# Block-sparse attention and a top-2 mixture of experts: the sums of the exponentials shared out between GpSimd and VectorE, with further sums ahead of TensorE

## The chip, the cores and the metric

The kernel runs on one core of a Trainium2 chip. The core has TensorE for matrix products (PE in the profile; PEld is its loading of weights), VectorE (DVE), ScalarE (ACT) and GpSimd (POOL), each with its own queue of instructions, executed in order; SyncE (SP) issues DMA transfers only. ScalarE and GpSimd issue some transfers too. The metric is the time on the device in microseconds, the median of several runs; lower is better.

## The reference, cut to what matters

Four batches of eight heads attend over 768 rows of width 64. Then each of the 3072 rows, 512 wide, goes through its two best of eight experts.

```python
scores = scale * np.matmul(q, k.transpose(0, 1, 3, 2))
scores = np.where(mask, scores, -1000000000.0)
scores = scores - np.max(scores, axis=-1, keepdims=True)
attn = np.exp(scores)
attn = attn / (np.sum(attn, axis=-1, keepdims=True) + 1e-09)
attn_out = np.matmul(attn, v)
x = attn_out.transpose(0, 2, 1, 3).reshape(B * S, H * D)
# router: noisy logits of x, the two best experts of each row, their weights
# experts: out[row] += weight * (relu(x[row] @ w1[e]) @ w2[e])
```

What the change touches is the sum over the exponentials, the epsilon, and the maximum on its way into the exponent.

## The kernel before, in words

**Attention.** Two heads make a group. A head has six chunks of 128 keys, one for each step: 192 steps in all, written out by `Attention.steps`. In step n TensorE forms the transposed scores of one chunk against all 768 queries in two halves (tile `pe`, L237 and L238: high and low parts of q and k in float16, and the maximum and the mask as further columns of the second product). ScalarE turns them into exponentials (tile `p`, float32, L239, five buffers). Four steps later TensorE multiplies them with the values (tile `po`, L269).

The maximum of each query is found ahead of time. TensorE forms the scores the other way round (tile `pm`, two buffers, L208), VectorE reduces them (`m`, L215), up to eleven chunks ahead of the step. When a head's six maxima are there, `max_end` writes them, scaled and in float16, into a column of `qb` on VectorE (L222); one step later SyncE transposes `qb` into `q2` (L225), which L238 of that head uses. The first heads have less lead than eleven chunks.

**The sums.** `add` (L257) lets GpSimd add the exponentials of two neighbouring chunks into a tile `acc`, 128 x 768: three pair sums for each head. `sums` (L280) then lets TensorE add those three, and the 128 keys within each, by matmuls with a constant column: four matmuls of 192 columns for each of the three, beside each other in four column groups of the array. ScalarE copies the result (`sb`, L297), VectorE transposes it (L300), adds epsilon (`rc`, L302) and takes the reciprocal (L305). TensorE turns the product with the values back (L310), VectorE scales it (`xr`, L313), ScalarE and GpSimd split it into two float16 parts (`x`, L322, L324).

Buffers tie the engines: an exponential needs a free `p`, freed by its pair sum and its product with the values; a product `pm` needs the reduction two before it done.

**Other work in the same queues.** GpSimd forms the low parts of k and q for later groups (L175, L179). The router of each batch runs in pieces in the steps of the next: some forty small VectorE instructions, then 48 writes to the table `slots` over the four batches, twelve a batch, each a small memset and an indirect DMA on GpSimd (L651, L652). The third batch's twelve stand closer together than those of the first two. Near the end of the attention GpSimd gathers the rows of the first expert (L771).

**Experts.** Units of up to 816 rows: two products on TensorE (L823, L843), ScalarE and VectorE between them, results scattered by GpSimd (L890). The fourth batch's router and table writes run beside the first unit.

Of the kernel before, what the change touches and what calls it, by code (L numbers as in the profile page):

```python
# [9 lines left out]
F32 = mybir.dt.float32  # L10
# [29 lines left out]
class Attention:  # L40
# [10 lines left out]
    PPB = 5  # L51
    LA = 4

    def __init__(self, tc, q, k, v, sampled):
# [10 lines left out]
        self.now = 0  # L65

# [98 lines left out]
    def split(self, g, part, h=None):  # L165
# [6 lines left out]
        if part == 0:  # L172
            nc.scalar.activation(ka[:, hs, :, 0:D], kx[:, hs], AF.Copy)
            self.later(1 if self.now else 0,
                       lambda: nc.gpsimd.tensor_sub(ka[:, hs, :, D:], kx[:, hs], ka[:, hs, :, 0:D]))  # L175
        elif part == 1:
            nc.scalar.activation(qa[:, hs, :, 0:D], qx[:, hs], AF.Copy)
            self.later(1 if self.now else 0,
                       lambda: nc.gpsimd.tensor_sub(qb[:, hs, :, 0:D], qx[:, hs], qa[:, hs, :, 0:D]))  # L179
        elif part == 2:  # L180
# [36 lines left out]
    def max_end(self, n):  # L217
        g, h, t = self.where(n)
        r = self.st[g]
        if t == self.T - 1:  # L220
            qb = self.nat[g % 2][2]
            self.nc.vector.tensor_scalar(qb[:, h, :, 64 + self.NB], r["m", h], -1.0 / 64.0, LNS / 8.0,  # L222
                                         op0=ALU.mult, op1=ALU.add)
# [27 lines left out]

    def add(self, n):

        g, h, c = self.where(n)
        if c % 2:
            acc = self.pp.tile([P, self.T, P], F32, name="acc", bufs=4)
            self.nc.gpsimd.tensor_add(acc, self.st["p", n - 1], self.st["p", n])  # L257
            self.st[g].setdefault(("acc", h), []).append(acc)
# [24 lines left out]
    def av_end(self, n, part, on_group):  # L283
# [6 lines left out]
        if part == "copy":  # L290
            xo = r["xo", h] = self.sm.tile([P, 3 * P], F32, name="xo", bufs=2)
            nc.scalar.activation(xo, r.pop(("o", h)), AF.Copy)
        elif part == "sums":
            self.sums(r, h)
        elif part == "sums out":
            sb = r["sb", h] = self.sm.tile([P, 32 * T], F32, name="sb", bufs=2)
            nc.scalar.activation(sb, r.pop(("b", h))[:, 0:32 * T], AF.Copy)  # L297
        elif part == "sum":
# [3 lines left out]
            nc.vector.tensor_scalar(r["rc", h], st.rearrange("p (t i) -> p t i", t=T)[:, :, 0],  # L302
                                    1e-9 * math.exp(LNS) / XS, None, op0=ALU.add)
        elif part == "inverse":
            nc.vector.reciprocal(r["rc", h], r["rc", h])  # L305
# [22 lines left out]
    def start(self, mi):  # L328
# [37 lines left out]
        self.load(0, nc.scalar, "v")  # L366
# [7 lines left out]
        self.plan = {0: [(self.load, 2)], 3: [(self.load, 1, None, "v")], 4: [(self.load, 3)],  # L374
# [5 lines left out]
    def steps(self, on_group, background):  # L380
        NSTEP, LM, LA, GT = self.NSTEP, self.LM, self.LA, self.G * self.T
        for n in range(NSTEP + LA + 7 + self.ROWLATE):
            g, i = divmod(n, GT)
            self.now = n
            for f in self.todo.pop(n, []):
                f()
# [30 lines left out]
            self.av_end(j - 2, "inverse", on_group)  # L417
            if 0 <= n - 1 < NSTEP:
                self.add(n - 1)
            self.st.pop(("p", j - 1), None)  # L420
# [11 lines left out]
class Router:  # L432
# [73 lines left out]
    def run(self, b, ps):  # L506
# [19 lines left out]
        nc.vector.tensor_copy(lc, pv)  # L526
        yield
        lg = tile([P, T, 16], F32, "lg")
        nc.vector.tensor_tensor(lg, lc[:, :, 0:16], lc[:, :, 16:], op=ALU.add)
        yield  # L530
        z = tile([P, T, E], F32, "z")
        sc = 1.0 / (XS * WS)
        nc.vector.tensor_scalar(z, lg[:, :, E:], sc, 88.0, op0=ALU.mult, op1=ALU.min)
        for _ in range(self.HO):
            yield
        u = tile([P, T, E], F32, "u")
        nc.scalar.activation(u, z, AF.Exp)
        yield
        w = tile([P, T, E], F32, "w")
        nc.scalar.activation(w, u, AF.Copy, bias=1.0)  # L540
        yield
        lw = tile([P, T, E], F32, "lw")
        nc.scalar.activation(lw, w, AF.Ln)
        for _ in range(self.HO):
            yield

        iw = tile([P, T, E], F32, "iw")
        nc.vector.reciprocal(iw, w)
        yield
        r1 = tile([P, T, E], F32, "r1")  # L550
        nc.vector.scalar_tensor_tensor(r1, w, -1.0, u, op0=ALU.add, op1=ALU.subtract)
        yield
        nc.vector.tensor_tensor(r1, r1, iw, op=ALU.mult)
        yield
        nc.vector.tensor_tensor(lw, lw, r1, op=ALU.subtract)
        yield
# [605 lines left out]
```

## Time and profile before

| | us |
|---|---|
| median of 3 runs | 1045.05 |
| lowest and highest of them | 1043.16, 1046.9 |
| the profiled execution | 1044.98 |
| its span on the core | 1042.9 |
| TensorE busy | 971.7 |
| VectorE busy | 497.9 |
| GpSimd busy | 488.3 |
| ScalarE busy | 370.0 |

The profile is one execution recorded by the hardware. The span is shorter than the time of the execution by 2.1 us that lie around it. The attention's steps take until about 447 us, the experts the rest. A line of a group gives source line, engine, operation, output and input tiles, the count, then busy us and the mean ns of one, then the idle time ahead of it and what ended it. A line of a stretch gives its bounds and length, then busy time of PE, PEld, DVE, ACT and POOL with counts of instructions, TensorE's granted clock, the DMA engines' share and GB/s. A line of the timeline gives start, length, engine, line, operation, and in brackets the idle time ahead and what ended it. In the profile a float32 matmul counts as two instructions.

### The profile page before, as it was taken

To read this page: it belongs to the slowest core of one execution; us is meant where nothing else is said; L and a number is where in the kernel's file an instruction comes from. 1 tells how busy PE (TensorE), PEld (TensorE's weight loads), DVE (VectorE), ACT (ScalarE), POOL (GpSimd) and SP (SyncE) were. 2 spreads that over 40 slices of the span, in tenths; PEclk is the share of its full clock that TensorE was granted. 3 is DMA by queue.
4 is the path that set the end of the run, shared out by engine and by line. 5 is a ranking of instruction groups with operands and counts; after the bars stand their busy time and mean duration, and the time that the engine had idled before them with its cause. 6 is when DMAs were issued, how large, how long until landed. Compare 5 with 4: busy or idle time off the path is not lost. (4 is left out here: it accounts for less than half of the span.)

```text
span 1042.9 us, 15840 instructions
## 1 busy us (share of the span) xinstructions
PE 971.7 (93%) x6057; PEld 467.1 (45%) x6057; DVE 497.9 (48%) x870; ACT 370.0 (35%) x763; POOL 488.3 (47%) x474
## 2 busy tenths in 40 slices
PE   3899999999999997989789999999999999999993
PEld 1344444444444443455454454454454544544541
DVE  7465557766877686355314424234144242341220
ACT  2455555555555654543213114032032130320200
POOL 2466665787679768735344142261241422502211
PEclk9899999999999998999899999999999999999997
DMA  8969986777677753755598639359187393581200
GB/s 204 169 145 253 235 200 145 134 155 146 144 145 145 149 110 77 177 175 113 152 223 207 176 102 230 111 138 243 55 191 185 103 222 117 138 192 51 65 33 33
DMA packets 238503, 156.09 MB, mean 150 GB/s; under 512 B 173026, under 2 KB 214242, under 8 KB 238417
## 3 DMA queue, kind: packets, MB, share of 16 engines
q1 hardware_dynamic: 207264, 91.45, 42.1%
q0 software_dynamic: 14256, 39.58, 13.6%
q10 hardware_dynamic: 16896, 23.95, 8.3%
q8 instruction: 49, 0.80, 0.3%
q14 instruction: 38, 0.30, 0.1%
HBM read 79.62 MB, written 26.32 MB: 102 GB/s over the span
## 5 line engine op out<-in xcount | busy, mean ns | idle before, releaser
L239 ACT ACTIVATE p<-pe 128x384 f32<-128x384 f32 x384 | 187.6, 491 | 191.1 <-PE pe L238 170.0
L215 DVE TENSOR_REDUCE m<-pm 128x1 f32<-128x768 f32 x192 | 181.8, 953 | 116.9 <-PE pm L208 116.5
L890 POOL DMA_INDIRECT out_dram<-y,mt x56 | 60.6, 1082 | 320.9 <-DVE y L884 215.0
L257 POOL TENSOR_TENSOR acc<-p,p 128x768 f32<-128x768 f32 x96 | 174.1, 1816 | 63.7 <-ACT p L239 54.7
L828 ACT ACTIVATE hh<-ph 128x408 f16<-128x408 f32 (+2 forms) x136 | 66.7, 491 | 337.9 <-PE ph L823 278.5
L269 PE MATMUL po<-p,vx 128*64 128x384 f32 x768 | 160.6, 511 | 0.0
L237 PE MATMUL pe<-q,k 128*128 128x384 f16 x384 | 129.1, 336 | 7.6 <-ACT p L239 4.8
L829 DVE SCALAR_TENSOR_TENSOR hl<-ph,hh 128x408 f16<-128x408 f32 (+2 forms) x136 | 76.0, 559 | 123.7 <-ACT hh L828 122.9
L238 PE MATMUL pe<-q,k 128*128 128x384 f16 x384 | 126.7, 330 | 7.9 <-DMA q<-qb 7.9
L823 PE MATMUL ph<-xta,w1hb 128*128 128x408 f16 x512 | 114.6, 348 | 11.3 <-DVE hl L829 6.9
L884 DVE SCALAR_TENSOR_TENSOR y<-py,mt,pv 128x512 f32<-128x512 f32 (+1 forms) x55 | 41.2, 748 | 168.5 <-PE py L843 151.6
L843 PEld LDWEIGHTS <-hh 128*128 128x128 f16 x768 | 74.9, 98 | 98.1 <-issue 10.8
L208 PE MATMUL pm<-k,q 88*128 88x384 f16 x384 | 98.6, 341 | 13.0 <-DMA k<-kb 10.6
L823 PE MATMUL ph<-xtb,w1ha 128*128 128x408 f16 (+1 forms) x448 | 91.1, 325 | 4.6 <-DVE hl L829 3.7
L237 PEld LDWEIGHTS <-k 128*128 128x128 f16 x384 | 37.2, 97 | 118.8 <-issue 105.0
L843 PE MATMUL py<-w2ha,hh 128*128 128x512 f16 x192 | 73.8, 384 | 6.2 <-DVE y L884 6.2
L823 PEld LDWEIGHTS <-w1hb 128*128 128x128 f16 x512 | 51.3, 100 | 53.2 <-issue 17.0
L789 POOL DMA_INDIRECT pv<-out_dram,gi x56 | 59.1, 1055 | 34.1 <-issue 18.5
L843 PE MATMUL py<-w2ha,hl 128*128 128x512 f16 x192 | 73.6, 383 | 1.0 <-DVE hl L829 1.0
L823 PEld LDWEIGHTS <-w1ha 128*128 128x128 f16 x576 | 56.0, 98 | 40.9 <-issue 5.8
L843 PE MATMUL py<-w2la,hh 128*128 128x512 f16 x192 | 73.6, 384 | 0.0
L843 PE MATMUL py<-w2hb,hh 128*128 128x512 f16 x192 | 72.8, 379 | 0.0
(177 smaller groups left out, 1263.2 us busy)
## 6 DMA issues: line engine op xcount, KB each, us to landing
wraw<-in_moe_w_dram SPq DMA_DIRECT2D x64, 512.0 KB, 5.9
q<-q SPq DMA_DIRECT2D x32, 192.0 KB, 3.4
vx<-in_v_dram ACTq DMA_DIRECT2D x16, 384.0 KB, 4.2
out_dram<-zero ACTq DMA_DIRECT2D x8, 768.0 KB, 5.7
x_rows<-x SPq DMA_DIRECT2D x16, 384.0 KB, 4.0
raw_k<-in_k_dram ACTq DMA_DIRECT2D x14, 384.0 KB, 4.7
raw_q<-in_q_dram ACTq DMA_DIRECT2D x14, 384.0 KB, 5.3
k<-k SPq DMA_DIRECT2D x17, 192.0 KB, 2.7
```

Source lines behind the costliest of these rows:

```text
L208: self.nc.tensor.matmul(pm[:, c, 0:384], r["q3"][0:K, h, t, :], r["k2"][0:K, h, 3 * c:3 * c + 3, :], start=True, stop=True)
L215: self.nc.vector.tensor_reduce(self.st[g]["m", h][:, t:t + 1], pm[:, :, 0:384], axis=AX.XY, op=ALU.max)
L237: nc.tensor.matmul(pe[:, 0:384], r["k1"][:, h, c, :], r["q1"][:, h, t, :], start=True, stop=False)
L238: nc.tensor.matmul(pe[:, 0:384], r["k2"][:, h, c, :], r["q2", h][:, t, :], start=False, stop=True)
L239: nc.scalar.activation(p32[:, t].rearrange("p t c -> p (t c)"), pe[:, 0:384], AF.Exp, scale=0.125)
L257: self.nc.gpsimd.tensor_add(acc, self.st["p", n - 1], self.st["p", n])
L269: self.nc.tensor.matmul(po[s * D:(s + 1) * D], r["v"][:, h, c, :], p32[:, 3 * s:3 * s + 3].rearrange("p t c -> p (t c)"), start=c == 0, st ...
L823: nc.tensor.matmul(ph[:, b, 0:m], w[wt][:, kb, fs], r["xt"][:, kb, a, o:o + m], start=i == 0, stop=i == last)
L828: nc.scalar.activation(hv, ph[:, b, 0:m], AF.Relu)
L829: nc.vector.scalar_tensor_tensor(self.hl[:, f, o:o + m], ph[:, b, 0:m], 0.0, hv, op0=ALU.max, op1=ALU.subtract)
L843: nc.tensor.matmul(py, h[:, f, o], w[x][:, f, :], start=i == 0, stop=i == last)
L890: nc.gpsimd.indirect_dma_start(out=self.out, out_offset=bass.IndirectOffsetOnAxis(ap=r["mt"][0:m, c, 0:1], axis=0), in_=y[0:m], in_offset= ...
```

## The change

Each engine gets a running count of its work in ns (`busy`), raised by `work` wherever instructions are issued, and held at no more than 4000 behind the step times 2000. `plus` puts a sum on whichever of GpSimd (at 1800) and VectorE (at 1050) would end earlier by the count. A new function `merge` adds, one step after a pair sum, the second and the third `acc` of a head into the first, but only if an engine would end by the count a whole step of 2000 before the current one; such a further sum leaves TensorE one tile less to add. `acc` has five buffers for four.

The scaled maximum moves from VectorE to ScalarE, a step later, and the transpose behind it another step. Epsilon comes in as the bias of ScalarE's copy, so VectorE's addition goes, and the reciprocal reads the transposed tile. The first group's load of the values is issued in step 1 and not ahead of step 0.

```diff
+    def plus(self, out, a, b):
+        u, w = self.busy["v"] + 1050, self.busy["p"] + 1800
+        if out is a and min(u, w) > self.now * self.STEP - self.SPARE:
+            return False
+        if w <= u:
+            self.nc.gpsimd.tensor_add(out, a, b)
+            self.work(p=1800)
+        else:
+            self.nc.vector.tensor_add(out, a, b)
+            self.work(v=1050)
+        return True
     def add(self, n):
         g, h, c = self.where(n)
+        accs = self.st[g].setdefault(("acc", h), [])
         if c % 2:
-            acc = self.pp.tile([P, self.T, P], F32, name="acc", bufs=4)
-            self.nc.gpsimd.tensor_add(acc, self.st["p", n - 1], self.st["p", n])
-            self.st[g].setdefault(("acc", h), []).append(acc)
+            acc = self.pp.tile([P, self.T, P], F32, name="acc", bufs=5)
+            self.plus(acc, self.st["p", n - 1], self.st["p", n])
+            accs.append(acc)
+    def merge(self, n):
+        g, h, c = self.where(n)
+        accs = self.st[g]["acc", h]
+        if c in (3, 5) and self.plus(accs[0], accs[0], accs[-1]):
+            accs.pop()
...
-            self.nc.vector.tensor_scalar(qb[:, h, :, 64 + self.NB], r["m", h], -1.0 / 64.0, LNS / 8.0,
-                                         op0=ALU.mult, op1=ALU.add)
-            self.later(self.Q2LATE, lambda: self.nc.sync.dma_start_transpose(
-                out=d, in_=qb[:, h].rearrange("p t c -> p (t c)")))
+            def send():
+                self.nc.scalar.activation(qb[:, h, :, 64 + self.NB], r["m", h], AF.Copy, scale=-1.0 / 64.0, bias=LNS / 8.0)
+                self.later(self.Q2LATE, lambda: self.nc.sync.dma_start_transpose(
+                    out=d, in_=qb[:, h].rearrange("p t c -> p (t c)")))
+            self.later(1 if n >= self.T + self.XM else 0, send)
...
-            nc.scalar.activation(sb, r.pop(("b", h))[:, 0:32 * T], AF.Copy)
+            nc.scalar.activation(sb, r.pop(("b", h))[:, 0:32 * T], AF.Copy, bias=1e-9 * math.exp(LNS) / XS)
...
-            nc.vector.tensor_scalar(r["rc", h], st.rearrange("p (t i) -> p t i", t=T)[:, :, 0],
-                                    1e-9 * math.exp(LNS) / XS, None, op0=ALU.add)
-        elif part == "inverse":
-            nc.vector.reciprocal(r["rc", h], r["rc", h])
+            nc.vector.reciprocal(r["rc", h], st.rearrange("p (t i) -> p t i", t=T)[:, :, 0])
...
-        self.load(0, nc.scalar, "v")
...
-        self.plan = {0: [(self.load, 2)], 3: [(self.load, 1, None, "v")], 4: [(self.load, 3)],
+        self.plan = {0: [(self.load, 2)], 1: [(self.load, 0, None, "v")], 3: [(self.load, 1, None, "v")], 4: [(self.load, 3)],
...
+            for e in self.busy:
+                self.busy[e] = max(self.busy[e], n * self.STEP - self.AHEAD)
+            self.work(a=1000, v=950)
...
             if 0 <= n - 1 < NSTEP:
                 self.add(n - 1)
+            if 0 <= n - 2 < NSTEP:
+                self.merge(n - 2)
```

The rest of the diff calls `work` with numbers for the router's, the weights' and the gathers' instructions; the router's on VectorE count three times.

As built, 69 of the 96 pair sums stand on GpSimd and 27 on VectorE; 53 further sums are made, 41 on GpSimd and 12 on VectorE. Of the 32 heads 23 leave TensorE one tile, seven leave two, two leave three.

On TensorE, the block of sums of the first head, before (`pe` with `inv` is the block, `q` and `k` the scores around it):

```order
L238 MATMUL pe<-q_293,k_97 128x384
L280 MATMUL pe<-acc,inv 32x192 x12
L237 LDWEIGHTS k_156
L237 MATMUL pe<-q_178,k_156 128x384
L238 LDWEIGHTS k_97
```

and now:

```order
L246 MATMUL pe<-q_292,k_97 128x384
L313 MATMUL pe<-acc,inv 32x192 x4
L245 LDWEIGHTS k_156
L245 MATMUL pe<-q_178,k_156 128x384
L246 LDWEIGHTS k_97
```

Twelve matmuls became four; nothing around them moved.

On GpSimd, the last part of the third batch's table writes (`slots` is the table, `acc` a pair sum, `x` the low half of a finished head), before:

```order
L692 MEMSET xg 128x1024
L651 MEMSET r_spacer 1x1
L652 DMA slots<-r_pay,r_sl 28160x2
L651 MEMSET r_spacer 1x1
L652 DMA slots<-r_pay,r_sl 28160x2
L257 TENSOR_TENSOR acc<-p_4700,p_4726 128x768
L651 MEMSET r_spacer 1x1
L652 DMA slots<-r_pay,r_sl 28160x2
L324 TENSOR_TENSOR x<-xr,x 128x6x64
L651 MEMSET r_spacer 1x1
L652 DMA slots<-r_pay,r_sl 28160x2
L257 TENSOR_TENSOR acc<-p_4769,p_4801 128x768
```

and now on VectorE, where `m` is the reduction of the scores and `sbt`, `rc`, `xr` belong to the end of a head:

```order
L221 TENSOR_REDUCE m<-pm 128x1 x3
L274 TENSOR_TENSOR acc<-p_4532,p_4557 128x768
L221 TENSOR_REDUCE m<-pm 128x1 x2
L274 TENSOR_TENSOR acc<-p_4601,p_4633 128x768
L334 STREAM_TRANSPOSE sbt<-sb 128x192
L336 RECIPROCAL rc<-sbt 128x6
```

These are the two pair sums of the fence before it (buffers have other numbers in the two programs): they left GpSimd's queue for VectorE's. In the twelve table writes of each of the first two batches, GpSimd had nine pair sums between the first and the last write; now it has three pair sums and three further ones there, and VectorE has nine sums in the same part.

On GpSimd, the end of the attention behind the last gather (`xg`), before:

```order
L771 DMA xg<-x_rows,gi 128x1024
L257 TENSOR_TENSOR acc<-p_5067,p_5089 128x768
L257 TENSOR_TENSOR acc<-p_5115,p_5132 128x768
L257 TENSOR_TENSOR acc<-p_5154,p_5167 128x768
L324 TENSOR_TENSOR x<-xr,x 128x6x64
L257 TENSOR_TENSOR acc<-p_5179,p_5195 128x768
L257 TENSOR_TENSOR acc<-p_5221,p_5237 128x768
```

and now (`acc<-acc` is a further sum):

```order
L836 DMA xg<-x_rows,gi 128x1024
L271 TENSOR_TENSOR acc<-p_4899,p_4921 128x768
L271 TENSOR_TENSOR acc<-acc 128x768
L271 TENSOR_TENSOR acc<-p_4939,p_4956 128x768
L271 TENSOR_TENSOR acc<-acc 128x768
L271 TENSOR_TENSOR acc<-p_4978,p_4991 128x768
L355 TENSOR_TENSOR x<-xr,x 128x6x64
L271 TENSOR_TENSOR acc<-p_5004,p_5020 128x768
L271 TENSOR_TENSOR acc<-acc 128x768
L271 TENSOR_TENSOR acc<-p_5038,p_5054 128x768
L271 TENSOR_TENSOR acc<-acc 128x768
```

Four further sums stand between the pair sums of the last two heads; one pair sum ahead of the gather moved to VectorE.

More of the change, by code (lines that the diff above doesn't have):

```diff
@@ L65, in __init__ @@
         self.now = 0
+        self.busy = {"v": 0.0, "p": 0.0, "a": 0.0}
     def open(self, ctx, early):
@@ L504, in rows, with run @@
             "(p t) c -> p t c", p=P), x.rearrange("p t a c -> p t (a c)"))
-    def run(self, b, ps):
+    def run(self, b, ps, work):
         nc, T, D, pool = self.nc, self.T, self.D, self.pool
@@ L526, in run @@
         nc.vector.tensor_copy(lc, pv)
+        work(v=325)
         yield
@@ L529, in run @@
         nc.vector.tensor_tensor(lg, lc[:, :, 0:16], lc[:, :, 16:], op=ALU.add)
+        work(v=160)
         yield
@@ L537, in run @@
         nc.scalar.activation(u, z, AF.Exp)
+        work(a=215)
         yield
@@ L540, in run @@
         nc.scalar.activation(w, u, AF.Copy, bias=1.0)
+        work(a=215)
         yield
@@ L543, in run @@
         nc.scalar.activation(lw, w, AF.Ln)
+        work(a=215)
         for _ in range(self.HO):
@@ L548, in run @@
         nc.vector.reciprocal(iw, w)
+        work(v=250)
         yield
@@ L560, in run @@
         nc.vector.scalar_tensor_tensor(ny, lg[:, :, 0:E], sc, lw, op0=ALU.mult, op1=ALU.add)
+        work(v=110)
         yield
@@ L567, in run @@
                 if t % 3 == 2:
+                    work(v=230)
                     yield
@@ L570, in run @@
         nc.vector.tensor_tensor(dl, mx[:, :, 1], mx[:, :, 0], op=ALU.subtract)
+        work(v=70)
         yield
@@ L573, in run @@
         nc.vector.tensor_copy(ef, mi[:, :, 0:2])
+        work(v=70)
         yield
@@ L580, in run @@
             nc.vector.memset(self.R[:, 0:1], 0.0)
+        work(v=160)
         yield
@@ L585, in run @@
         nc.vector.tensor_copy(Rh, self.R[:, 0:E])
+        work(v=180)
         yield
@@ L588, in run @@
         nc.vector.tensor_scalar(z0, ef, 0.0, None, op0=ALU.is_equal)
+        work(v=70)
         yield
@@ L592, in run @@
         nc.scalar.activation(ex, dl, AF.Exp)
+        work(a=180)
         for _ in range(self.YL if last else self.YN):
@@ L606, in run @@
         nc.vector.tensor_tensor(A, A, po[:, :, None, :].to_broadcast([P, T, 2, E]), op=ALU.mult)
+        work(v=230)
         yield
@@ L609, in run @@
         nc.vector.tensor_reduce(pos, A, axis=AX.X, op=ALU.add)
+        work(v=160)
         yield
@@ L622, in run @@
         nc.vector.scalar_tensor_tensor(s1, ve, float(C), pos, op0=ALU.mult, op1=ALU.add)
+        work(v=140)
         yield
@@ L628, in run @@
         nc.vector.tensor_scalar(den, ex, 1.0, 1e-9, op0=ALU.add, op1=ALU.add)
+        work(v=140)
         yield
@@ L631, in run @@
         nc.vector.reciprocal(den, den)
+        work(v=170)
         yield
@@ L636, in run @@
         nc.vector.tensor_scalar(pay[:, :, 0, 1], den, GS, None, op0=ALU.mult)
+        work(v=140)
         yield
@@ L641, in run @@
         nc.vector.tensor_tensor(pay[:, :, 1, 1], ex, pay[:, :, 0, 1], op=ALU.mult)
+        work(v=140)
         yield
@@ L994, in on_group @@
         if kb == DM // P - 1:
-            jobs.append(router.run(b, lambda: psum[0]()))
+            jobs.append(router.run(b, lambda: psum[0](), lambda v=0, p=0, a=0: att.work(3 * v, p, a)))
     psum = [att.psum]
@@ L1026, in gather_early @@
         ex.gather(0, c)
+        att.work(p=1040)
     at(NS - AHEAD, ex.meta, 0)
```

25 lines of the change are left out of this document (23 added, 2 removed).

## Prediction

> **What bounds the kernel now.** I read the busy line, the busy time by stretch, then the groups.
>
> ```profile
> span 1042.9 us, 15840 instructions
> PE 971.7 (93%) x6057; PEld 467.1 (45%) x6057; DVE 497.9 (48%) x870; ACT 370.0 (35%) x763; POOL 488.3 (47%) x474
> 200.00:245.00 45.00, 44.86 (x319) 19.35 (x318) 32.70 (x42) 26.34 (x61) 40.75 (x46) 1.00 0.76 150
> 385.00:425.00 40.00, 34.62 (x214) 14.09 (x213) 27.14 (x47) 17.98 (x41) 28.23 (x36) 0.91 0.53 113
> 425.00:446.00 21.00, 20.71 (x153) 8.49 (x155) 4.59 (x8) 10.76 (x26) 18.35 (x14) 1.00 0.74 168
> ```
>
> In 200 to 245 us, the middle of the attention, TensorE (third number) is busy 44.86 of 45.00 us at full clock. GpSimd has 40.75 there, VectorE 32.70, ScalarE 26.34. So TensorE sets the pace, and its matmuls are worth their full time; GpSimd stands close behind. Only 385 to 425 falls out, with 34.62 of 40. The change edits the attention alone. The experts' first matmul follows its last one (a row below), so I let all behind the attention move with it, unchanged.
>
> **The sums of the exponentials on TensorE.**
>
> ```profile
> 200.41 1.51 PE L269 MATMUL po<-p,vx 128*64 128x384 f32 x8
> 201.86 0.34 PE L237 MATMUL pe<-q,k 128*128 128x384 f16 x1
> 203.01 1.18 PE L280 MATMUL pe<-acc,inv 128*32 128x192 f32 x24
> 204.13 0.34 PE L237 MATMUL pe<-q,k 128*128 128x384 f16 x1
> 205.21 0.87 PE L269 MATMUL po<-p,vx 128*64 128x384 f32 x4
> 206.01 0.34 PE L237 MATMUL pe<-q,k 128*128 128x384 f16 x1
> L280 PE MATMUL pe<-acc,inv 128*32 128x192 f32 x768 | 37.8, 330 | 0.0
> L257 POOL TENSOR_TENSOR acc<-p,p 128x768 f32<-128x768 f32 x96 | 174.1, 1816 | 63.7 <-ACT p L239 54.7 <-DMA q<-q 2.1 <-DMA x_rows<-x 2.1
> ```
>
> A head's block holds three sums of four matmuls. From its start to the next matmul it takes 204.13 - 203.01 = 1.12 us. A double block of L269 takes 1.45, a single one 0.80: a block costs 0.15 fixed and 0.65 for each part. By that pattern the sums cost 0.15 + 3 x 0.325, which is the 1.12 seen. All blocks together are 37.8 us busy, 0.394 for each of 96 sums, the upper bound.
>
> The order of the changed kernel makes 53 further sums, 41 on GpSimd and 12 on VectorE. 53 sums less on TensorE are **17.2 us** (53 x 0.325), at most 20.9.
>
> **The stall at the third batch.** It is the one large gap of TensorE between the start and the experts.
>
> ```profile
> 402.96 1.81 POOL L257 TENSOR_TENSOR acc<-p,p 128x768 f32<-128x768 f32 x1
> 404.80 0.87 ACT L239 ACTIVATE p<-pe 128x384 f32<-128x384 f32 x2 [6.50 <-POOL r_spacer L651]
> 405.34 0.48 PE L237 MATMUL pe<-q,k 128*128 128x384 f16 x1 [4.57 <-ACT p L239]
> 406.58 0.52 PE L237 MATMUL pe<-q,k 128*128 128x384 f16 x1
> 411.42 0.34 PE L237 MATMUL pe<-q,k 128*128 128x384 f16 x1
> ```
>
> Beside the twelve table writes GpSimd's pair sum ends only at 404.77. It holds two of the five buffers of exponentials, so ScalarE stands 6.50 us and TensorE 4.57 us. Then TensorE's matmuls take 0.52 instead of 0.34 us until about 410, some 5 us at two thirds of the speed, which I put at 1.8 us: the stall costs 6.4. In the new order this very pair sum and the next one go to VectorE, which takes two of GpSimd's 1.816 us out of the queue. What is late next is GpSimd's third pair sum behind the same writes; with 3.6 us less ahead of it, it comes about when ScalarE wants the buffer. I take **6 us**, between 0 and 6.4.
>
> **The work moved to VectorE.** Without a wait, its price comes from two shapes.
>
> ```profile
> L351 DVE TENSOR_TENSOR ka<-raw_k,ka 128x384 f16<-128x384 f32 x2 | 1.1, 554 | 0.3 <-ACT ka L350 0.3
> L735 DVE SCALAR_TENSOR_TENSOR w1la<-wraw,w1ha 128x1024 f16<-128x1024 f32 x16 | 19.5, 1223 | 19.7 <-ACT w1ha L734 19.7
> L215 DVE TENSOR_REDUCE m<-pm 128x1 f32<-128x768 f32 x192 | 181.8, 953 | 116.9 <-PE pm L208 116.5
> L222 DVE TENSOR_SCALAR qb<-m 128x6 f16<-128x6 f32 x32 | 23.6, 738 | 1.0
> L302 DVE TENSOR_SCALAR rc<-sbt 128x6 f32<-128x6 f32 x32 | 17.7, 553 | 1.1
> L297 ACT ACTIVATE sb<-pe 128x192 f32<-128x192 f32 x32 | 10.4, 325 | 0.6 <-PE pe L280 0.6
> ```
>
> 384 columns take 0.554, 1024 take 1.223; on the line between them 768 take 0.955. VectorE gets 27 pair sums and 12 further ones: 39 x 0.955 = 37.2 us. It loses L222 and L302, 23.6 + 17.7 = 41.3. So its total hardly changes, and no stretch of it sits on the path.
>
> But six numbers for each partition should not take 738 ns. These rows say why:
>
> ```profile
> 199.47 1.85 POOL L257 TENSOR_TENSOR acc<-p,p 128x768 f32<-128x768 f32 x1 [1.24 <-ACT p L239]
> 199.62 1.74 DVE L641 TENSOR_TENSOR r_pay<-r_ex,r_pay 128x6 f32<-128x6 f32 x1
> 407.81 6.54 DVE L222 TENSOR_SCALAR qb<-m 128x6 f16<-128x6 f32 x1
> 408.08 5.35 POOL L257 TENSOR_TENSOR acc<-p,p 128x768 f32<-128x768 f32 x3
> 413.38 0.91 POOL L324 TENSOR_TENSOR x<-xr,x 128x384 f16<-128x384 f32 x1
> L302 DVE TENSOR_SCALAR rc<-sbt 128x6 f32<-128x6 f32 x4 | 5.7, 1416 | 0.1
> ```
>
> The six-column product at 199.62 stands until GpSimd's sum ends; L222 at 407.81 stands through four GpSimd instructions in a row. The last row is L302 in 200 to 245 alone, 1.416 us each. So a VectorE instruction of this kind, one with two SBUF inputs among them, waits for GpSimd; the new pair sums are of that kind. I price the wait in a busy stretch by the last row, at about 1.1 us: nine VectorE sums fall there, 9 x (0.955 + 1.1) = 18.5. With L302 (5.7) and L222 (three, at the mean 2.2) gone, VectorE has 32.7 - 7.9 + 18.5 = 43.3 of about 43.5 us. It just fits.
>
> GpSimd in that stretch has nine sums between the table writes and gets six, 40.75 - 3 x 1.816 = 35.3. No row shows GpSimd held up by VectorE. If each VectorE sum stops it for its own length, 9 x 0.955 = 8.6 comes back and it needs 43.9 plus some 2 us of gaps between its instructions, 2.4 over the 43.5 (45 less some five sums at 0.325). So this stretch, and its twin one batch later, may idle TensorE by 0 to 2.5 us each; I take 1 each, **2 us lost**.
>
> [...]
>
> **The tail.** The last heads get their further sums from GpSimd while TensorE has less to do for each step.
>
> ```profile
> 433.73 5.36 POOL L257 TENSOR_TENSOR acc<-p,p 128x768 f32<-128x768 f32 x3
> 439.97 1.81 POOL L257 TENSOR_TENSOR acc<-p,p 128x768 f32<-128x768 f32 x1
> 443.02 1.81 POOL L257 TENSOR_TENSOR acc<-p,p 128x768 f32<-128x768 f32 x1 [1.24 <-ACT p L239]
> 445.87 1.18 PE L280 MATMUL pe<-acc,inv 128*32 128x192 f32 x24
> 449.04 0.72 PE L823 MATMUL ph<-xta,w1ha 128*128 128x320 f16 x4 [1.51 <-DVE xr L313]
> ```
>
> GpSimd is busy 18.35 of 21 us from 425 on; its last sum ends 1.0 us before TensorE's block at 445.87. The new order has four further sums there and one pair sum less: 3 x 1.816 = 5.4 us more, and TensorE's two last blocks come 1.3 earlier. 5.4 + 1.3 - 1.0 - 1.24 (GpSimd's gap at 443) = 4.5; part may go into idle time ahead of 425. Nothing covers it, as the experts' matmuls stand behind that block: **4 us lost**, 0 to 5.
>
> **Small edits.** 32 scaled maxima on ScalarE take at most 0.325 each (the L297 row), 10 us on an engine with 26 of 45; they stand ahead of an exponential, and their maximum is reduced a step before. The q2 transpose is issued a step later; in the steady run that leaves four steps until its use. Epsilon as a bias costs nothing. The first values' load moves behind the first step:
>
> ```profile
> 16.20 0.44 ACTq L149 DMA_DIRECT2D vx<-in_v_dram  x1
> 31.98 0.87 PE L269 MATMUL po<-p,vx 128*64 128x384 f32 x4
> 39.32 0.48 PE L238 MATMUL pe<-q,k 128*128 128x384 f16 x1 [4.33 <-DMA q<-qb]
> ```
>
> Its consumer runs at 31.98. If it lands late, that wait comes out of the 4.33 us of the next one. The same bytes go through until 39, so I take 0, from 2 gained to 2 lost.
>
> **The sum.** -17.2 - 6 + 2 + 4 = -17.2. The profiled execution took 1044.98 us (span 1042.9 and 2.1 around it), beside a median of 1045.05: 1044.98 - 17.2 = **1028**.
>
> **The rivals.**
>
> *GpSimd becomes the bound.* Each VectorE sum stops GpSimd for its own length: 39 x 0.955 = 37 us come onto GpSimd, beside 14 sums more (110 for 96), 25 us. For it: 40.75 of 45. Against it: much of the attention is less crowded. Both stretches then lose 2.5, half of the 6 us stall stays, the tail takes 5, and 3 us are lost in ordinary groups: 17.2 - 2.5 - 5 + 3 - 3 = 10 gained at the best; with a second such loss where its queue stays full, 7: about 1038. [...]
>
> *VectorE is starved, and the kernel gets slower.* L222's 6.54 us shows that GpSimd's back-to-back sums let VectorE wait for all of them. Two buffers of scores cover two steps of about 2.1 us (201.86, 204.13 and 206.01 above begin one each) less one reduction of 0.953, 3.2. A pair sum starved like that idles TensorE by 6.5 + 0.955 - 3.2 = 4.2. Five such cases eat the gain of 17; ten of the eighteen VectorE sums in the two stretches give 42 - 17 = 25 slower, 1070. Against it: with GpSimd as full, the stretch of 200 to 245 shows waits near 1.2.
>
> *The further sums come too late.* The change doesn't do what it says: TensorE's block waits for the longer chain of every head and gives its shorter time back. A further sum is 1.816; TensorE would lose 0.5 a head, 16 us, and the time stays near 1044. Against it: they are issued only where the count has an engine ahead, and two steps before the block.
>
> *More than counted.* Each sum is worth its 0.394 busy us, and the tail finds room: 20.9 + 6.4 = 27, 1018.
>
> **How the numbers follow.** Forecast 0.62 (1020 to 1036), GpSimd bound 0.16, starved 0.08, too late 0.06, more 0.08. The measurement tells 0.3% from no change, 3.1 us. Faster: 0.62 + 0.08 + 0.14 of the GpSimd case = 0.84. Same: 0.06 + 0.02 = 0.08. Slower: 0.08. The range leaves out the starved case, half of the late one and part of the best: 1019 to 1041.
>
> **What would show it.** The block L280 should fall from 1.12 to about 0.47 where one sum is left; TensorE should stay near 45 of 45 in the stretches of the table writes; the gap of 4.57 should be gone, and a wait for a GpSimd sum of some 4 us should stand ahead of the last block. I am wrong if TensorE shows many waits for VectorE's reductions or for ScalarE behind a pair sum, or if pair sums on VectorE take well over 2 us.

## The result and the profile after

The changed kernel takes 1030.99 us (median of 19 runs, 1025.88 to 1038.47), the kernel before on the same chip 1042.94 (19 runs, 1032.87 to 1052.68). The ratio is 0.9914, 95% interval [0.9891, 0.9936]: 9.0 us faster (6.7 to 11.4) where 17 were forecast. The medians lie 12 us apart; ratios and clocks here leave out executions in a slower state, over 1.5% above the fastest of the same kernel (two of the kernel before here, two in the last experiment). 1031 lies 3 us above the forecast and inside its range. The profiled execution took 1029.09 us, its span is 1027.3.

First the busy line of the page, then the busy time by stretch, in the columns of the prediction (TensorE is the third number, GpSimd the last with an x, the granted clock behind it):

```profile
span 1027.3 us, 14952 instructions
PE 952.4 (93%) x5633; PEld 452.3 (44%) x5633; DVE 506.3 (49%) x845; ACT 374.4 (36%) x795; POOL 518.5 (50%) x488
200.00:245.00 45.00, 45.00 (x276) 18.19 (x276) 32.92 (x42) 28.88 (x70) 38.13 (x40) 1.00 0.81 156
345.00:385.00 40.00, 36.97 (x251) 15.25 (x252) 29.41 (x75) 20.10 (x52) 25.26 (x24) 0.91 0.45 96
385.00:425.00 40.00, 37.14 (x241) 14.54 (x237) 18.95 (x26) 21.47 (x52) 35.33 (x35) 1.00 0.77 150
425.00:446.00 21.00, 15.24 (x100) 8.27 (x101) 3.51 (x9) 6.38 (x15) 17.37 (x14) 0.92 0.45 99
```

The table-write stretch of 200 to 245, for which I had feared a wait, is full: 45.00 of 45, and so is its twin one batch later, 300 to 345. TensorE stands idle elsewhere, in 345 to 385 and behind 385. The next rows are the block of a head with one sum left and the matmul behind it, the group of all blocks, and the experts' first matmul:

```profile
412.57 0.53 PE L313 MATMUL pe<-acc,inv 128*32 128x192 f32 x8
413.04 0.34 PE L245 MATMUL pe<-q,k 128*128 128x384 f16 x1
L313 PE MATMUL pe<-acc,inv 128*32 128x192 f32 x344 | 20.8, 335 | 6.5 <-POOL acc L271 6.5
438.32 1.25 PE L888 MATMUL ph<-xta,w1ha 128*128 128x320 f16 x4 [1.30 <-DVE xr L344]
```

A block now takes 413.04 - 412.57 = 0.47 us, and all together 20.8 where 37.8 stood: 17.0 less. Yet the experts start only 449.04 - 438.32 = 10.7 us earlier. What ate the rest is in the waits of TensorE from 46 us to there, by line and releaser (us in total, times, the longest):

```profile
PE pe L313 <- POOL acc L271: 6.5, 3, 3.4
PE pm L214 <- DVE m L221: 4.3, 5, 2.4
PE pe L245 <- DVE xr L344: 3.7, 3, 1.5
PE ph L888 <- DVE xr L344: 1.3, 1, 1.3
PE pe L245 <- ACT p L247: 0.8, 2, 0.6
```

16.6 us, where the kernel before had 7.9, of which 4.57 were the stall at the third batch. That stall is gone. New are the first row, the sums of GpSimd that come late, and the second and third: VectorE's reductions of the scores and its scaling of a finished head. The waits one by one:

```profile
166.80 0.48 PE L214 MATMUL pm<-k,q 88*128 88x384 f16 x2 [0.61 <-DVE m L221]
172.95 0.49 PE L214 MATMUL pm<-k,q 88*128 88x384 f16 x2 [0.36 <-DVE m L221]
176.07 0.32 PE L245 MATMUL pe<-q,k 128*128 128x384 f16 x1 [1.51 <-DVE xr L344]
366.08 0.62 PE L214 MATMUL pm<-k,q 88*128 88x384 f16 x2 [2.38 <-DVE m L221]
367.36 0.48 PE L245 MATMUL pe<-q,k 128*128 128x384 f16 x1 [0.65 <-DVE xr L344]
426.06 0.53 PE L313 MATMUL pe<-acc,inv 128*32 128x192 f32 x8 [2.33 <-POOL acc L271]
436.00 0.53 PE L313 MATMUL pe<-acc,inv 128*32 128x192 f32 x8 [3.39 <-POOL acc L271]
```

The last two are the tail, 5.7 us, and with ScalarE's 0.63 at 421 it costs 6.4. The others come once in each of the first three batches: 2.5 us at 166 to 176, the same at 267 to 277, 3.0 at 366. Each time VectorE stands in a burst of the router's small instructions. VectorE, then GpSimd, in the first of them:

```profile
162.36 1.74 DVE L593 SCALAR_TENSOR_TENSOR r_r<-r_w,r_u 128x48 f32<-128x48 f32 x1
164.13 1.74 DVE L596 TENSOR_TENSOR r_r<-r_r,r_iw 128x48 f32<-128x48 f32 x1
165.80 0.94 DVE L221 TENSOR_REDUCE m<-pm 128x1 f32<-128x768 f32 x1
```

```profile
162.23 1.81 POOL L271 TENSOR_TENSOR acc<-acc 128x768 f32<-128x768 f32 x1 [1.27 <-DVE acc L274]
163.99 1.82 POOL L271 TENSOR_TENSOR acc<-p,p 128x768 f32<-128x768 f32 x1
165.76 0.92 POOL L355 TENSOR_TENSOR x<-xr,x 128x384 f16<-128x384 f32 x1
```

Products of 48 columns end with GpSimd's sum beside them and take 1.74 us each; at 166.67 the next one of that size, with no sum beside it, takes 0.19. The reduction at 165.80 stands behind both, and it is the one for which TensorE waits at 166.80. In the kernel before, L551 is the same instruction as L593:

```profile
L551 DVE SCALAR_TENSOR_TENSOR r_r<-r_w,r_u 128x48 f32<-128x48 f32 x4 | 1.7, 433 | 0.0
```

```profile
L593 DVE SCALAR_TENSOR_TENSOR r_r<-r_w,r_u 128x48 f32<-128x48 f32 x4 | 4.8, 1193 | 0.0
L596 DVE TENSOR_TENSOR r_r<-r_r,r_iw 128x48 f32<-128x48 f32 x4 | 4.8, 1201 | 0.1
```

So the waits of VectorE for GpSimd, which I had priced for the sums, fell for the most part on other instructions.

### The profile page after: what moved, and what is told of

The parts are those of the page before. It is cut to its first block, busy times and chain, and to the rows that moved or that the text cites. A ratio compares the mean times of both kernels' runs of the same rounds, so it can differ in the third digit from the quotient of the medians.

```text
span 1027.3 us, 14952 instructions
## 1 busy us (share of the span) xinstructions
PE 952.4 (93%) x5633; PEld 452.3 (44%) x5633; DVE 506.3 (49%) x845; ACT 374.4 (36%) x795; POOL 518.5 (50%) x488
## 5 line engine op out<-in xcount | busy, mean ns | idle before, releaser
L271 POOL TENSOR_TENSOR acc<-p,p 128x768 f32<-128x768 f32 x69 | 125.0, 1812 | 26.6 <-ACT p L247 26.4
L894 DVE SCALAR_TENSOR_TENSOR hl<-ph,hh 128x408 f16<-128x408 f32 (+2 forms) x136 | 76.0, 560 | 125.9 <-ACT hh L893 125.9
L246 PE MATMUL pe<-q,k 128*128 128x384 f16 x384 | 126.5, 329 | 3.3 <-DMA q<-qb 3.3
L888 PE MATMUL ph<-xta,w1hb 128*128 128x408 f16 x512 | 111.2, 340 | 10.1 <-DMA xta<-xg 6.4
L214 PE MATMUL pm<-k,q 88*128 88x384 f16 x384 | 98.4, 341 | 18.4 <-DMA k<-kb 10.7
L271 POOL TENSOR_TENSOR acc<-acc 128x768 f32<-128x768 f32 x41 | 74.2, 1811 | 19.8 <-DVE acc L274 17.0
L854 POOL DMA_INDIRECT pv<-out_dram,gi x56 | 57.8, 1031 | 34.5 <-issue 17.8
```

The costliest lines, as they stand in the source:

```text
L214: self.nc.tensor.matmul(pm[:, c, 0:384], r["q3"][0:K, h, t, :], r["k2"][0:K, h, 3 * c:3 * c + 3, :], start=True, stop=True)
L246: nc.tensor.matmul(pe[:, 0:384], r["k2"][:, h, c, :], r["q2", h][:, t, :], start=False, stop=True)
L271: self.nc.gpsimd.tensor_add(out, a, b)
L888: nc.tensor.matmul(ph[:, b, 0:m], w[wt][:, kb, fs], r["xt"][:, kb, a, o:o + m], start=i == 0, stop=i == last)
L894: nc.vector.scalar_tensor_tensor(self.hl[:, f, o:o + m], ph[:, b, 0:m], 0.0, hv, op0=ALU.max, op1=ALU.subtract)
```

## The experiments

They ran on four chips, and none of them behaves like that of the first comparison: the kernel before takes 1065.64 to 1068.84 us there (medians). In the one profile of it all of the difference lies behind the attention (622.11 us for 593.86), and its mean granted clock over the executions is 0.974 to 0.976. From here on a block is the four matmuls with which TensorE adds one tile of a head's sums. Three times stand for each: the experts' first matmul in the profile (the end of the attention), the ratio to the kernel before on the same chip, and the mean granted clock of the timed executions.

| run | first experts' matmul | ratio, interval | clock (before beside it) |
|---|---|---|---|
| no further sums | 439.37 | 0.9936 [0.9907, 0.9965] | 0.976 (0.976) |
| none near a burst | 434.71 | 0.9906 [0.9868, 0.9943] | 0.970 (0.976) |
| maximum on VectorE | 436.92 | 0.9997 [0.9971, 1.0023] | 0.969 (0.976) |
| tail on VectorE | 439.36 | 0.9991 [0.9960, 1.0022] | 0.971 (0.976) |
| the change itself | 436.82 | 0.9977 [0.9954, 0.9999] | 0.969 (0.975) |
| sums only where free | 426.59 | 0.9944 [0.9914, 0.9974] | 0.971 (0.975) |
| further sums, blocks kept | 450.75 | 1.0048 [1.0018, 1.0078] | 0.976 (0.975) |
| no further sums, blocks left out | 425.48 | 0.9893 [0.9854, 0.9931] | 0.970 (0.975) |
| the change again | 435.59 | 0.9977 [0.9953, 1.0002] | 0.969 (0.975) |
| whole program later | 445.19 | 1.0100 [1.0054, 1.0147] | 0.967 (0.974) |

The kernel before, profiled on one of these chips, had its experts' first matmul at 443.69. Of the 5.35 us to the first profile's 449.04, 2.7 lie in the waits of the start (21.6 there, 18.9 here).

**Without the further sums.** The count still places the pair sums (82 on GpSimd, 14 on VectorE), TensorE gets three blocks for every head.

```
-        if c in (3, 5) and self.plus(accs[0], accs[0], accs[-1]):
+        if False:
```

> All 96 pair sums stay, shared out by the count; no further sum is made, so TensorE adds three tiles for each head again (53 x 0.325 = 17.2 us more on TensorE than in the changed kernel). If the further sums are worth their time on TensorE and cost only what the profile of the changed kernel shows as new gaps (8.0 us behind VectorE's work for the router, 6.5 us ahead of the last blocks), the experts' first matmul comes at 438.3 + 17.2 - 14.5 = 441, and both kinds of gaps are gone, the gap of 4.57 us of the kernel before too. Rival, that the gaps come from the moved maximum or the pair sums on VectorE and not from the further sums: the 8 us of gaps stay and it comes at 449.

The blocks are back, and the waits are gone. Its group of blocks, and 345 to 385 us:

```profile
L313 PE MATMUL pe<-acc,inv 128*32 128x192 f32 x768 | 38.1, 330 | 0.8 <-POOL acc L271 0.8
345.00:385.00 40.00, 39.85 (x320) 17.57 (x319) 26.02 (x73) 22.37 (x56) 23.70 (x19) 1.00 0.70 134
```

TensorE waits 4.2 us from 46 us on, where the change has 15.7 to 16.6. With 17 us more of blocks the attention ends only 2.6 to 3.8 us after that of the change. So the waits come with the further sums, which give back some 14 of their 17 us inside the attention. VectorE has 13 pair sums fewer here as well, and the small instructions still wait at times (L593 takes 991 ns in the mean), but what is queued behind them no longer holds TensorE up. The attention ends 4.3 us before that of the kernel before, where the change ends 6.9 before it (profiles of two chips): about the stall at the third batch (4.1 us there), which is gone. That fits the new places of the pair sums, though the small edits are in this run too. In time it stands at 0.9936, the change on two other chips at 0.9977; the intervals overlap, but a gain in time from the further sums doesn't show on these chips.

**No further sum near a burst.** It is skipped when VectorE has under 1.1 us in hand; 46 are left.

```
-        if out is a and min(u, w) > self.now * self.STEP - self.SPARE:
+        if out is a and (min(u, w) > self.now * self.STEP - self.SPARE or u > self.now * self.STEP - 1100):
```

> Further sums are skipped where VectorE's count is high, that is beside the router's work: 46 instead of 53, seven on GpSimd less. Theory 1, the router's small VectorE instructions wait for GpSimd's further sums: the gaps of TensorE in 160 to 180, 260 to 280 and 360 to 370 us (2.5, 2.5, 3.0) go, TensorE works 2.3 us more, the experts' first matmul comes 5 us earlier, at about 433. Theory 2, the moved maximum on ScalarE passes VectorE's lateness on: the gaps stay at 2 us or more each and it comes 2 us later, at about 440.

TensorE's waits of the first and the third burst:

```profile
170.96 0.48 PE L214 MATMUL pm<-k,q 88*128 88x384 f16 x2 [0.43 <-DVE m L221]
178.11 0.32 PE L245 MATMUL pe<-q,k 128*128 128x384 f16 x1 [1.45 <-DVE xr L344]
367.00 0.32 PE L245 MATMUL pe<-q,k 128*128 128x384 f16 x1 [0.34 <-DVE xr L344]
```

The third burst falls from 3.0 to 0.34 us, the first from 2.5 to 1.9, and the second like it: the wait for xr stays, against the theory. The attention ends at 434.71 where the theory had 433, seven blocks more on TensorE included. That is only 0.9 to 2.1 us ahead of the change on two other chips, with a start that took 2.3 longer than in one of them.

**The scaled maximum back on VectorE.** The rival to the sums as the cause of the waits was ScalarE, which now stands in its order until a maximum is there (up to 6.0 us at the third burst).

```
-                self.nc.scalar.activation(qb[:, h, :, 64 + self.NB], r["m", h], AF.Copy, scale=-1.0 / 64.0, bias=LNS / 8.0)
+                self.nc.vector.tensor_scalar(qb[:, h, :, 64 + self.NB], r["m", h], -1.0 / 64.0, LNS / 8.0,
+                                             op0=ALU.mult, op1=ALU.add)
...
-            self.later(1 if n >= self.T + self.XM else 0, send)
+            send()
```

> The scaled maximum goes back to VectorE and the transpose a step earlier; all else as changed. Theory 1 (waits for GpSimd's further sums): the gaps beside the router's work stay or grow, since one more VectorE instruction of that kind waits; the experts' first matmul comes at 438 or some 3 us later. Theory 2 (ScalarE's wait for the maximum, 18.1 us in all, 5.97 the longest): the gap at 366 us shrinks from 3.0 to under 1, the others to 1 or less, and it comes 3 to 5 us earlier.

The bursts keep their waits within 0.14 us: 0.65, 0.34 and 1.52, the same again, 2.38 and 0.79. ScalarE's wait is a witness of the burst, not its cause. The time is that of the kernel before and no better than that of the change; the interval doesn't tell the two apart.

**The tail's further sums on VectorE.** The four of the last nine steps.

```
-        if w <= u:
+        if w <= u and not (out is a and self.now > self.NSTEP - 9):
```

> The four further sums of the last two heads go to VectorE, which is nearly idle there; nothing else differs. If GpSimd's queue is what TensorE waits for ahead of the last blocks (2.33 and 3.39 us), both waits go to under 0.5 and the experts' first matmul comes 5 us earlier, at about 433. Rival, that the exponentials themselves come late: the waits stay above 2 us.

I missed this one. TensorE at the place, and VectorE ahead of it:

```profile
423.49 0.48 PE L245 MATMUL pe<-q,k 128*128 128x384 f16 x1 [4.93 <-DVE xr L344]
437.07 0.53 PE L313 MATMUL pe<-acc,inv 128*32 128x192 f32 x8 [0.64 <-DVE acc L274]
```

```profile
420.42 2.54 DVE L274 TENSOR_TENSOR acc<-acc 128x768 f32<-128x768 f32 x1 [5.31 <-POOL acc L271]
422.89 0.55 DVE L344 TENSOR_TENSOR xr<-pe,rc 128x384 f32<-128x384 f32 x1
```

The wait ahead of the last block falls to 0.64, but VectorE stands 5.31 us for a pair sum of GpSimd, then 2.54 in its own sum, and xr is queued behind it. TensorE loses 4.93 us for a result that had nothing to do with the sum. VectorE took the two in the order of its queue, and so the moved sum brought its wait along.

**The sums only where both have room.** The burst rule, and no further sum in the last nine steps; 42 are left.

```
-        if out is a and min(u, w) > self.now * self.STEP - self.SPARE:
+        if out is a and (min(u, w) > self.now * self.STEP - self.SPARE or u > self.now * self.STEP - 1100
+                         or self.now > self.NSTEP - 9):
```

> No further sum where VectorE has under 1.1 us in hand (as in e2_no_burst), and none in the last nine steps of the attention, where GpSimd's sums stood back to back. The theory (the two waits of 2.3 and 3.4 us ahead of the last block's matmuls are GpSimd's further sums): both fall under 0.7 us, four blocks of 0.65 us in place of 0.33 us add 1.3 us, and the experts' first matmul comes 2 to 4 us earlier than with the burst rule alone: 431 to 433, ratio 0.986 to 0.991 against the kernel before. The rival (the pair sums alone keep GpSimd late there, or something else follows, as when the sums went to VectorE): waits of 2 us or more stay ahead of the last block, first experts' matmul 435 to 437, ratio 0.990 to 0.994.

The group of blocks and the end of the attention:

```profile
L313 PE MATMUL pe<-acc,inv 128*32 128x192 f32 x432 | 24.4, 333 | 0.7 <-POOL acc L271 0.7
426.59 0.72 PE L888 MATMUL ph<-xta,w1ha 128*128 128x320 f16 x4 [1.30 <-DVE xr L344]
```

The attention is better than either theory had it: the blocks wait 0.7 us in all, and the attention ends 10.2 us before that of the change on the same chip and 17.1 before that of the kernel before. Eleven sums fewer cost 3.6 us of blocks and save 9.5 of waits; the start took 1.1 more in this profile, and the rest is clock, 1.00 throughout this attention and 0.99 in that of the change. The time is not: 0.9944 where the theory had 0.986 to 0.991 and the rival 0.990 to 0.994. The row behind the attention:

```profile
426.59:1057.30 630.71, 563.20 (x3108) 291.16 (x3108) 206.12 (x337) 128.33 (x205) 184.38 (x188) 0.96 0.52 134
```

That is 8.6 us longer than the 622.11 of the kernel before on this chip, at the same busy time of TensorE (563.74 there). TensorE waits more, for VectorE's `hl` alone (L894, L829 before) 25.0 us in place of 16.1. The run without further sums has 29.3 of that wait, so it may be scatter; one profile of each doesn't tell.

In time it gains 6.4 us on the kernel before (1059.29 beside 1065.67), the change 3.0 (1062.66). Of the kernels that do the whole work it is the best one timed beside the change, though the two intervals overlap; the one with the burst rule alone stands at 0.9906, from four executions on another chip.

**The first values early.** Only this load is put back.

```
+        self.load(0, nc.scalar, "v")
...
-        self.plan = {0: [(self.load, 2)], 1: [(self.load, 0, None, "v")], 3: [(self.load, 1, None, "v")], 4: [(self.load, 3)],
+        self.plan = {0: [(self.load, 2)], 3: [(self.load, 1, None, "v")], 4: [(self.load, 3)],
```

> The first group's values are loaded ahead of step 0 again, as before the change; the rest is the changed kernel. The theory (this transfer is what the first transposes waited behind before): TensorE's wait at the start is back at 4 to 4.5 us, where the changed kernel had 2.1, and the experts' first matmul is at 440 to 441. The rival (that wait moves with the order of other transfers): the start wait is 1 to 3.7 us as in the other variants, first experts' matmul 437 to 439.

```profile
40.37 0.48 PE L246 MATMUL pe<-q,k 128*128 128x384 f16 x1 [4.88 <-DMA q<-qb]
```

The old wait for the transpose is back, and the experts' first matmul is at 441.99, 5.2 us after that of the change on this chip. The kernel before, which loads early too, waited there 0.60 on this chip and 4.33 in the first profile: what sets its length is not shown, and two profiles don't give its mean.

**The change itself, and the kernel before, on another chip.**

```
(no edit; both kernels as they are)
```

> The changed kernel itself, beside the kernel before on the chip of this call. The theory (the dense stretch saves TensorE work, but a denser TensorE is granted less clock later): the experts' first matmul stands at 438 to 439 as in the first profile, 10 to 11 us earlier than the kernel before, while the mean granted clock lies 0.004 to 0.006 under that of the kernel before on the same chip, and the time ratio is then 0.994 to 0.998. The rival (the clock is not affected by the change): the two mean clocks agree within 0.002 and the ratio is 0.989 to 0.993, as in the first comparison.

> The kernel before, for its profile on the chip of this call. Both theories: experts' first matmul at 448 to 450, gap at the third batch's table writes 4.5 us. If the granted clock answers to the denser attention, the clock lost behind the first experts' matmul is 5 us or more below that of the changed kernel's profile of this call; if not, within 3 us of it.

The attention gains 6.9 us, the time 3.0 by the medians (the interval reaches from no change to 0.46%), so the size measured first doesn't hold on this chip. The attention of the kernel before ends at 443.69, not at 448 to 450 as both theories had it; its stall at the third batch is 4.1 us. One row for the attention, one for all behind it; before, then the change:

```profile
0.00:443.69 443.69, 416.18 (x2950) 178.34 (x2950) 290.40 (x533) 241.41 (x559) 301.79 (x286) 1.00 0.75 161
443.69:1065.80 622.11, 563.74 (x3108) 293.05 (x3108) 205.28 (x337) 128.10 (x205) 184.44 (x188) 0.95 0.53 136
```

```profile
0.00:436.82 436.82, 402.30 (x2526) 164.80 (x2526) 301.68 (x508) 246.21 (x591) 333.77 (x300) 0.99 0.77 164
436.82:1063.20 626.38, 566.30 (x3108) 293.32 (x3108) 205.66 (x337) 128.22 (x205) 184.61 (x188) 0.95 0.52 135
```

The part behind the attention, the same 3108 matmuls, takes 626.38 in place of 622.11 us, 4.3 longer: TensorE is busy 2.6 longer and waits about 1.3 longer. Over the executions the mean clock is 0.9685 beside 0.9747. If all of the time followed the clock, that would be 0.0062 x 1063 = 6.6 us. From execution to execution of the same kernel, though, 0.001 less of mean clock goes with only about 0.56 us more (an estimate, fitted over the executions on the four chips), which makes 3.5, near the 3.9 us by which the time gains less than the attention.

Where in the execution that clock is lost is not shown. Summed over stretches of 5 us (one less the granted clock, times the length), the two profiles lose 28.3 us behind the attention before and 29.9 with the change, and 1.7 and 5.3 in it. The 1.6 us more behind the attention are within the 3 that the expectation set for a clock that does not answer to the denser attention. The next runs ask what the mean clock follows.

**Further sums made, blocks kept.** For each block saved, the first one is multiplied once more into the columns that the real chain then starts afresh.

```
+        for acc in accs[0:1] * (3 - len(accs)):
+            for j in range(4):
+                q = slice(32 * j, 32 * j + 32)
+                self.nc.tensor.matmul(pb[q, 0:32 * self.T], self.inv, acc[:, :, q], start=True, stop=True,
+                                      tile_position=(0, 32 * j))
```

> The further sums are made as in the changed kernel, but TensorE multiplies three blocks for every head all the same: for each block that a sum has saved, the first one is multiplied once more into the same PSUM columns, which the real chain then starts afresh. TensorE's sums are back at about 37.8 us, while VectorE and GpSimd do the further sums. Theory P (the lower granted clock is the price of the further sums' work on VectorE and GpSimd): mean granted clock stays 0.004 to 0.007 under that of the kernel before, and the time is 1.005 to 1.015 of before. Theory Q (it is the price of the light 32-column matmuls that are gone): mean clock within 0.002 of the kernel before, time 0.995 to 1.004.

**No further sums, blocks left out.** On the kernel without further sums:

```
-        if False:
+        if c in (3, 5) and self.left > 0:
+            self.left -= 1
             accs.pop()
...
-            nc.scalar.activation(sb, r.pop(("b", h))[:, 0:32 * T], AF.Copy, bias=1e-9 * math.exp(LNS) / XS)
+            nc.scalar.activation(sb, r.pop(("b", h))[:, 0:32 * T], AF.Copy, scale=r.pop(("part", h)), bias=1e-9 * math.exp(LNS) / XS)
```

> No further sum is made, and TensorE leaves out 53 blocks of the sums (the first 53 of 64 that a further sum could save); the sum over the blocks that are left is scaled up on ScalarE, so the sums of exponentials are only estimates, a few per cent off, and the choice of experts shifts for some tokens. The pair sums lie as in e1_no_further. The experts' first matmul should come at 420 to 426, since neither VectorE nor GpSimd has the further sums. Theory P (the engines' work costs the clock): mean granted clock within 0.002 of the kernel before; time 0.977 to 0.985. Theory Q (the missing light matmuls cost the clock): mean clock 0.004 to 0.007 lower, time 0.984 to 0.990. If the experts' part fills up with waits whatever the clock does, the time is over 0.990.

**The change again**, beside these two on the same chip.

> The changed kernel once more, as the measure for the two others on the same chip: mean granted clock 0.004 to 0.006 under that of the kernel before and ratio 0.996 to 0.999 if the chip of this call throttles as in the second call; 0.989 to 0.993 with equal clocks if it is like the first comparison. Theories P and Q do not differ here.

The clocks fall where theory Q has them: 0.9758 with sums and blocks, 0.9700 with neither, 0.9691 for the change, 0.9752 for the kernel before (standard errors 0.0005 to 0.0013). It isn't the work of VectorE and GpSimd that costs the clock. With the blocks kept, the time is a little over Q's 1.004; the tail's waits are still there, 1.53 and 2.76 us. Nor is it that a shorter attention at full clock lowers the mean: 30 us of lost clock are 0.0281 of 1066 us and 0.0286 of 1048, so 18 us less of attention cost 0.0005.

**The whole program later.**

```
+        for _ in range(8):
+            nc.gpsimd.memset(r["k"], 0.0)
+            nc.gpsimd.memset(r["q"], 0.0)
```

> The changed kernel with 16 clears of the first tiles on GpSimd ahead of the first loads, which hold the whole program up by some 10 to 20 us before TensorE's first matmul; nothing else is changed, so the experts' first matmul comes that much later than its 436 to 438. The clock column counts this start as full speed. Theory Q (the blocks that TensorE no longer multiplies cost the later clock): the mean granted clock stays at 0.967 to 0.971, as in the two timings of the changed kernel, and the time is that kernel's plus the whole delay (1.007 to 1.017 of the kernel before). Theory S (the experts lose more the earlier they begin, whatever the reason for the early start): mean clock back at 0.974 to 0.977, and 4 to 6 us of the delay are not seen in the time (1.002 to 1.012).

TensorE starts at 21.45 in place of 10.71 us, 10.7 later. The clock stays low, 0.9673 beside 0.9737, and the time is 1.0100: 0.0123 more than that of the change, 13 us, the whole delay within the intervals. Theory S falls; an early start of the experts isn't what costs the clock.

**Where the clock goes stays open in part.** Part of it is plain: in 345 to 385 us of the change the clock is 0.91. It is 0.50 from 366.4 to 372.8, behind the wait of 2.38 us that ends at 366.08, and again from 438 to 441, behind that of 3.39 which ends at 436.00:

```profile
368.00:372.00 4.00, 4.00 (x13) 1.32 (x14) 2.82 (x5) 2.24 (x7) 1.57 (x1) 0.50 0.32 62
```

The matmuls of L246 behind 367 take 0.52 in place of 0.33 us. Behind the wait of 2.33 us that ends at 426.06 the clock stays at 1.00 (426 to 430); what sets the two apart no run here shows. Such waits are not the whole of it. The kernel with sums only where free waits 1.45 us at the most in its attention behind 46 us, which has a clock of 1.00 from start to end, and its mean is 0.9708 all the same. All kernels of the table that leave TensorE fewer blocks lie at 0.967 to 0.971, those that leave it every block at 0.974 to 0.976; what links a block of the attention to the mean clock no run here shows. On the first chip the changed kernel's mean is 0.979 and the kernel before's one profile 0.978, so there may be no such price there.

## Why the prediction came out as it did

Direction and range held, and the mechanism was the one named: TensorE's sums were worth their full time because TensorE was the bound (with the blocks kept, the attention ended 13.9 and 15.2 us after that of the change on two chips). The size was half, for terms that were missing or mis-sized. That the time came within 3 us of the forecast is in part luck: the three runs from which it starts have a median of 1045.05 where 19 have 1042.94, and 4.9 of the 15.6 us between the spans of the two profiles lie behind the attention, where nothing was changed.

- *Sums on TensorE, -17.2.* Right: 37.8 to 20.8 us, -17.0; the block 0.47 as forecast.
- *The stall at the third batch, -6.* Right: the gap of 4.57 and its slow clock (0.50 in 406 to 410 us) are gone, also without further sums (1.00 in 385 to 425). With them, a clock of 0.50 came back behind 366 us.
- *The two table-write stretches, +2.* Nothing was lost there (45.00 of 45 in both). Only four of the 39 sums on VectorE began while a `TENSOR_TENSOR` of GpSimd still had 0.1 us or more to run; GpSimd's L179 is L175 in the kernel before:

```profile
L274 DVE TENSOR_TENSOR acc<-p,p x27: 947/948/1982, 36.1 to 411.6; 128x768 f32<-128x768 f32 x27
L274 DVE TENSOR_TENSOR acc<-acc x12: 947/948/992, 54.0 to 410.7; 128x768 f32<-128x768 f32 x12
L175 POOL TENSOR_TENSOR ka<-raw_k,ka 128x384 f16<-128x384 f32 (+1 forms) x29 | 27.3, 940 | 39.3 <-ACT ka L173 39.3
L179 POOL TENSOR_TENSOR ka<-raw_k,ka 128x384 f16<-128x384 f32 (+1 forms) x29 | 29.9, 1033 | 41.4 <-ACT ka L177 41.3
```

  The median (the middle of three numbers) is 0.948, my 0.955 without the 1.1 of waiting; those four take 1.42 to 1.98. So VectorE is busy 32.92 us in 200 to 245 and not 43.3. That GpSimd is also held up by VectorE, which no row had shown, is so: L179 took 940 ns in the mean before and 1033 now, as 11 of its 28 of 384 columns go from 0.91 to 1.09 or more, up to 1.29. At 201.16, for one, it takes 1.28 us beside a VectorE sum that ends at 201.67. So each engine is slower beside the other at times. But that a VectorE sum stops GpSimd for its own length, 0.955 us, was my estimate; the most that L179 shows is 0.38 (1.29 in place of 0.91), and the 2.5 us for each stretch that I let follow did not come.
- *The step that failed.* "I price the wait in a busy stretch by the last row" took the wait from a small two-input instruction of VectorE and gave it to the sums alone. The router's small instructions, of the very kind of the row that I quoted, stayed out of the sum. With the further sums GpSimd is full beside them, the longest of them wait out a sum each (1.74 us beside 1.81), VectorE's reductions stand behind them, and TensorE loses 8.0 us in three places. That is the sign of being wrong that I had named, waits of TensorE for VectorE's reductions: there are five, 4.3 us in all. I had this as the starved rival, at 4.2 us for a stall, and gave it to the pair sums. Without further sums these waits vanish; that is shown. With seven of GpSimd's further sums left out beside the bursts, the third falls to 0.34 us but the first two only to 1.9 each, so what share GpSimd's further sums have in those two, and what share the other sums of the two engines, stays open.
- *The tail, +4.* Right in place, short in size: 6.4. I saw one block wait and not the one of the head ahead of it (2.33), behind the same queue.
- *Small edits, 0.* The start waits 2.4 us less (21.6 to 19.2) where I had given it up to 2; with the load in its old place a wait of 4.88 came back in one profile. ScalarE's copy with epsilon as its bias takes 327 ns in the median, without it 325.
- *The sum.* In the attention: -16.8 busy (419.02 to 402.23), -2.4 at the start, +8.7 of waits behind it, -10.5 of the 10.7 seen. That all behind the attention moves along unchanged held on the first chip within its scatter (593.9 to 589.0 us in two profiles) and failed on another, where that part took 4.3 us longer and the lower mean clock went with a smaller gain.

Of the rivals, GpSimd as the bound came nearest in time (1038; its 10 "at the best" takes the 2.5 us only once for the two stretches, and the 7 behind the 1038 takes it twice), yet by another way: GpSimd was never full in 200 to 245, with 38.13 of 45.

## What to carry to other kernels

When a wait is priced from a row, list every instruction of that row's kind in the stretch, not only the new ones: here, with GpSimd fuller, a small instruction of VectorE that was there already (L551, now L593) went from 433 to 1193 ns in the mean, and what was queued behind it came later. Ask, too, whether the engine that takes work off the bound is free until the result is due; here eleven sums fewer of 53 gave an attention 10 us shorter, of which 3.4 us showed in the time. And compare on more than one chip before a gain of 1% is called its size.

## What was not expected of the hardware

A six-column or 48-column instruction of VectorE with two inputs took up to 1.74 us beside a GpSimd sum of 1.81 to 1.86 and 0.14 to 0.21 alone. On four chips the mean granted clock was lower by 0.004 to 0.007 (some 2 to 4 us by the estimate above) wherever 42 to 53 blocks of 0.325 us were left out of the attention, whatever VectorE and GpSimd did and whenever the rest began.
